# Four merged weight loads and an earlier turn of x tile 2 at the start of a linear-attention and mixer kernel

## The chip, the cores and the metric

The kernel runs on one core of a Trainium2 chip. The metric is the device time of one launch in microseconds (us); 1 KB is 1024 bytes. The profiled execution's span runs from its first to its last instruction. The core has five engines with a program each: TensorE (PE, with its weight loads shown apart as PEld), VectorE (DVE), ScalarE (ACT), GpSimd (POOL) and SyncE (SP). SP and ACT issue DMA transfers from queues of their own.

## The reference

Two blocks work on the same x (2048 tokens of 640 values) and are mixed by a gate. Only the first lines matter for the change.

```python
g = _sigmoid((x * gate_w).sum(-1, keepdims=True))
qkv = (x @ wqkv)                       # 640 -> 3 * 640, split into q, k, v; 32 heads of 20
phi = lambda t: jnp.where(t > 0, t + 1, jnp.exp(t)) + 1e-6
pq, pk = phi(q), phi(k)
kv = jnp.einsum("bhsd,bhse->bhde", pk, v)
num = jnp.einsum("bhqd,bhde->bhqe", pq, kv)
...
b = _B_ref(x, w1, w2, w3, w4)          # layernorm, w1, gelu, token shifts, w2, layernorm, w3, gelu, w4
return g * a + (1 - g) * b
```

## The kernel before

The tokens are cut into 16 tiles of 128. A weight matrix with 640 rows is held as five slices of 128 rows, k = 0 to 4. A product for a token tile is five accumulating matmuls, one for each slice, into a PSUM bank: the turned x tile (`xT`) is the loaded operand, the slice of `wq` (512 columns) or of `wkg` (512 columns and 130 more, which hold the rest of wk, a column of ones and a column of the gate) is the one streamed.

The loads at the start are listed one after another. `load_x` puts x tiles on SP's queue; `load_wq` and `load_wk` (L683 to L687) put one slice each on the queue that they are given. SP's order is x0, x1, wq2, x2, wk0, x3, wk2, wk4, x4, then the DMA transposes `x_turn(3)`, the load of x5, `x_turn(4)` and so on; ACT's is wq0, wq1, wq3, wq4, wk1, wk3, and the last 128 columns of wq ("the tail of wq"). L285 issues every plain transfer, L281 every DMA transpose. Each load has its own semaphore, and whatever reads a slice waits for the semaphore of the transfer that wrote it.

x tiles 0, 1 and 2 are turned on PE instead: `t_x` transposes five blocks of 128 columns into a PSUM bank (L615) and DVE copies them into `xT` (L669). For tile 2 a sixth small matmul (L604, 128x5) goes into the same bank, with the gate's column, and DVE copies that into `wkg`; the first copy of tile 2 comes after it.

PE first runs warm-up matmuls on constants (L884), then `t_x(0)`, one more warm-up, and the two step lists. `q_three` makes the q tiles 0 to 2 and `k_two` the k tiles 0 and 1. Their lists name (tile, slice) pairs in PE's order, and (t, None) is the turn of tile t. `stream` issues them at L922 (512 columns) and L923 (the 130 more). When a tile's last slice is done, `phi` evicts it: an Exp on ACT (L660) into one of three slots of `Er`, then two DVE operations (L626, L643). A k tile has two more ACT operations, a copy of its last two columns and a sum of squares. From k tile 2 on each tile is one group of matmuls, `k_tile` or `q_tile` (L604).

All work after this is ordered by a planner (`_Items.run`): it holds streams of items and takes the next item by its estimated time, by its own model of the engines. `q_three` and `k_two` are one item each. Each engine runs its own list strictly in that order.

Of the kernel before, what the change touches and what calls it, by code (L numbers as in the profile page):

```python
# [11 lines left out]
D = 640  # L12
# [404 lines left out]
def _build(nc, A_x, A_wqkv, A_wo, B_w1, B_w2, B_w3, B_w4, gate_w, out, dbg=None, stop=None):  # L417
    sch = _Sched(nc)
# [79 lines left out]
    wkg = ra.alloc("wkg", [128, KD, NK], BF16)  # L498
    wq = ra.alloc("wq", [128, KD, D], BF16)
# [18 lines left out]
    def bank():  # L518
        best = None
        for k_ in range(nbanks[0]):  # L520
            b = (bank_rr[0] + k_) % nbanks[0]
            if b in bank_pend or b in bank_hold:
                continue
            lk = sch.locks.get(b)
            tfree = 0.0 if lk is None else sch.ev_time.get((lk[1].sem, lk[1].val), 1e18)
            if best is None or tfree < best[0]:
                best = (tfree, b)
        bank_rr[0] = best[1] + 1
        bank_pend.add(best[1])
        return best[1]  # L530
# [4 lines left out]
    def pair():  # L535
        best = None
        for k_ in range(4):
            q_ = (bank_rr[0] // 2 + k_) % 4
            tf = 0.0
            ok = True  # L540
            for b in (2 * q_, 2 * q_ + 1):
                if b in bank_pend or b in bank_hold:
                    ok = False
                lk = sch.locks.get(b)
                if lk is not None:
                    tf = max(tf, sch.ev_time.get((lk[1].sem, lk[1].val), 1e18))
            if ok and (best is None or tf < best[0]):
                best = (tf, 2 * q_)
        b = best[1]
        bank_rr[0] = b + 2  # L550
        bank_pend.update((b, b + 1))
        return b
# [36 lines left out]
    def pe(fn, reads, writes, cost=500.0):  # L589
        for w_ in writes:  # L590
            sp_, rl = sch.rects(w_)
            if sp_ == "ps":
                for (_p0, _p1, lo, hi) in rl:
                    for b in range(lo // PS_BANK, (hi - 1) // PS_BANK + 1):
                        bank_pend.discard(b)
        return sch.op("pe", fn, reads, writes, cost=cost)
# [83 lines left out]
    def load_x(t):  # L680
        dma_in(x_tok[:, t, :], x2[128 * t:128 * (t + 1), :], "x%d" % t)

    def load_wq(k, queue):  # L683
        sch.dma(queue, wq[:, k, 0:512], A_wqkv[128 * k:128 * (k + 1), 0:512], "wq%d" % k)

    def load_wk(k, queue):
        sch.dma(queue, wkg[:, k, 0:D], A_wqkv[128 * k:128 * (k + 1), D:2 * D], "wk%d" % k)  # L687

    def x_turn(t):
        sch.dma("sp", xT[:, :, 128 * t:128 * (t + 1)], x_tok[:, t, :], "trx%d" % (t % 4), transpose=True)  # L690
# [1 line left out]
    gwr = xn[:, 1, 0:128]  # L692
    dve(lambda e: e.memset(gwr, 0.0), [], [gwr])
    load_x(0)
    load_wq(0, "act")
    load_x(1)
    load_wq(1, "act")
    load_wq(2, "sp")
    load_wq(3, "act")
    load_x(2)  # L700
    load_wq(4, "act")
    load_wk(0, "sp")
    load_wk(1, "act")
    load_x(3)
    load_wk(3, "act")
    sch.dma("act", wq[:, :, 512:D], A_wqkv[:, 512:D].rearrange("(k p) f -> p k f", p=128), "wqt")
    load_wk(2, "sp")
    load_wk(4, "sp")
    load_x(4)
    x_turn(3)  # L710
    load_x(5)
# [65 lines left out]
    def t_x(t):  # L777
        for k0, k1 in ((0, 1), (1, KD)) if t < 2 else ((0, KD),):
            b = bank()
            tr_group(b, [x_tok[:, t, 128 * k:128 * (k + 1)] for k in range(k0, k1)])  # L780
            if t == 2:
                mm_group(ps[:, b, 448:448 + KD], [(gwr, ident[:, 0:KD])])
            for j0, j1 in {(1, 1): ((1, 3), (3, KD)), (2, 0): ((0, 2), (2, KD))}.get((t, k0), ((k0, k1),)):
                copy(dve, xT[:, j0:j1, 128 * t:128 * (t + 1)], psb(b, 128 * (j0 - k0), 128 * (j1 - k0)).rearrange("p (k c) -> p k c", k=j1 - j0))
            if t == 2:
                copy(dve, wkg[:, :, D + 1:D + 2], ps[:, b, 448:448 + KD].rearrange("p (k o) -> p k o", o=1))

    def phi(b, dst, after_exp=None, n=D):
        se = slot("E", 3)
        src = psf[:, 512 * b:512 * b + n]  # L790
        er = Er[:, se, 0:n]
        activation(er, src, ACTF.Exp)
        if after_exp is not None:
            after_exp()
        ts(dve, er, er, 1.0, EPS_PHI, ALU.min, ALU.add)
        return stt(dst, src, 1.0 + EPS_PHI, er, ALU.add, ALU.max)
# [79 lines left out]
    def warmup(cols, cyc):  # L876
        b = bank()
        one = nc.const_aps.tensor(1.0, [128, 512], BF16)
        steps = [512] * (cols // 512) + [128] * (cols % 512 // 128)

        def fn(e):
            ins = None
            for n in steps:
                ins = e.matmul(ps[:, b, 0:n], one[:, 0:128], one[:, 0:n], start=True, stop=True)  # L884
            return ins
        pe(fn, [], [ps[:, b, :]], cost=cols * cyc)
# [19 lines left out]
    def stream(order, w, n2, done):  # L906
        bs = {}
        for t in sorted({t for t, k in order if k is not None}):
            bs[t] = pair() if n2 else bank()
            bank_hold.update((bs[t], bs[t] + 1) if n2 else (bs[t],))  # L910
        for t, k in order:
            if k is None:
                if t is None:
                    warmup(256, 0.42)
                else:
                    t_x(t)
                continue
            b = bs[t]
            l = xT[:, k, 128 * t:128 * (t + 1)]

            def fn(e, l=l, b=b, k=k):
                ins = e.matmul(ps[:, b, 0:512], l, w[:, k, 0:512], start=(k == 0), stop=(k == KD - 1))  # L922
                return ins if not n2 else e.matmul(ps[:, b + 1, 0:n2], l, w[:, k, 512:512 + n2], start=(k == 0), stop=(k == KD - 1))  # L923
            pe(fn, [w[:, k, 0:512 + n2], l], [ps[:, b, 0:512]] + ([ps[:, b + 1, 0:n2]] if n2 else []), cost=272.0 if n2 else 216.0)
            if k == KD - 1:
                bank_hold.difference_update((b, b + 1) if n2 else (b,))
                done(t, b)

    def q_three():
        order = [(0, 0), (1, None), (0, 1), (1, 0), (1, 1), (0, 2), (1, 2), (0, 3), (1, 3), (2, None), (0, 4), (1, 4),  # L930
                 (2, 0), (2, 1), (2, 2), (2, 3), (2, 4)]
        stream(order, wq, 0, lambda t, b: phi(b, pq_tok[:, t + 1, 0:512], n=512))

    def k_out(t, b):
# [1 line left out]
        activation(junk[:, 0, :], x_tok[:, t, :], ACTF.Square, accum=st1[:, 1, t:t + 1])  # L936

    def k_two():
        stream([(0, 0), (0, 1), (0, 2), (1, 0), (0, 3), (1, 1), (1, 2), (0, 4), (1, 3), (1, 4)], wkg, 130, k_out)

    def addA(name, dur, fn, deps=()):
        IT.add("A", name, dur, fn, deps)
# [2 lines left out]
    addA(("tx", 0), 0.28, lambda: t_x(0))  # L945
    addA(("warm", 1), 0.0, lambda: warmup(WARM2, 0.42))
    addA(("q", 2), 3.24, q_three)
    addA(("k", 1), 2.72, k_two)
    addA(("k", 2), 1.36, lambda: k_tile(2))
    for i in range(3, NT + 2):  # L950
# [449 lines left out]
    order = IT.run(sch, hook)  # L1400
# [6 lines left out]
def bass_gated_mix__linear_attn_block__mixer_s_mlp__prompt_kernel(  # L1407
    nc, A_x, A_wqkv, A_wo, B_x, B_w1, B_w2, B_w3, B_w4, gate_w, out
):
    assert tuple(A_x.shape) == (1, S, D) and tuple(out.shape) == (1, S, D)  # L1410
    assert tuple(A_wqkv.shape) == (D, 3 * D) and tuple(A_wo.shape) == (D, D)
    assert tuple(B_w1.shape) == (D, D) and tuple(B_w2.shape) == (D, D)
    assert tuple(B_w3.shape) == (D, F) and tuple(B_w4.shape) == (F, D) and tuple(gate_w.shape) == (D,)
    _build(nc, A_x, A_wqkv, A_wo, B_w1, B_w2, B_w3, B_w4, gate_w, out)
# [28 lines left out]
```

## Time and profile before

| What | Value |
|---|---|
| Time, median of 3 | 259.3 us (258.84 to 259.4) |
| Profiled execution, its own time | 259.2 us |
| Its span | 257.9 us |
| First matmul on x (transpose, L615) | 3.68 us |
| First q step (L922) | 4.38 us |
| First k step (L922) | 8.96 us |
| First ACT table load; first Exp | 4.14 us; 7.73 us |
| First x transpose by DMA on SP | 8.75 us |
| HBM read, written | 12.04 MB, 2.62 MB |

Times in views are counted from the span's start. A line of the timeline gives start, duration, engine, line of the code, operation, output<-inputs and, in brackets, the idle time before it and what ended it. The queues' lines (SPq, ACTq) show the issue of a transfer, not its data; the DMA issues give the time from an issue's start to its landing.

### The profile page before, as it was taken

To read this page: it belongs to the slowest core of one execution; us is meant where nothing else is said; L and a number is where in the kernel's file an instruction comes from. 1 tells how busy PE (TensorE), PEld (TensorE's weight loads), DVE (VectorE), ACT (ScalarE), POOL (GpSimd) and SP (SyncE) were. 2 spreads that over 40 slices of the span, in tenths; PEclk is the share of its full clock that TensorE was granted. 3 is DMA by queue.
4 is the path that set the end of the run, shared out by engine and by line. 5 is a ranking of instruction groups with operands and counts; after the bars stand their busy time and mean duration, and the time that the engine had idled before them with its cause. 6 is when DMAs were issued, how large, how long until landed. Compare 5 with 4: busy or idle time off the path is not lost.

```text
span 257.9 us, 3904 instructions
## 1 busy us (share of the span) xinstructions
PE 255.1 (99%) x1478; PEld 126.7 (49%) x1478; DVE 144.8 (56%) x289; ACT 108.9 (42%) x224; POOL 90.9 (35%) x144
## 2 busy tenths in 40 slices
PE   8999999999999999999999999999999999999996
PEld 4555555544454545555444445444444744444744
DVE  2697888899964995589999300399700033200033
ACT  1587676651366868666854331001540100253100
POOL 5020499976952162677908000123200021300000
PEclk9999999999999999999999999999999999999999
DMA  7856699956637699372628630114130022200012
GB/s 226 226 135 114 188 137 177 262 109 126 127 76 79 125 399 293 84 100 56 121 49 117 123 60 3 31 25 127 36 17 0 3 52 80 102 1 3 0 20 102
DMA packets 57650, 26.50 MB, mean 103 GB/s; under 512 B 48884, under 2 KB 56221, under 8 KB 57632
## 3 DMA queue, kind: packets, MB, share of 16 engines
q1 hardware_dynamic: 54800, 21.87, 40.2%
q0 software_dynamic: 1168, 3.28, 5.8%
q10 hardware_dynamic: 1664, 1.11, 1.4%
q8 instruction: 11, 0.18, 0.3%
q14 instruction: 7, 0.06, 0.1%
HBM read 12.04 MB, written 2.62 MB: 57 GB/s over the span
## 4 chain that ended last, share of the span: by engine, by line
PE 99%; DVE 0%; issue 0%
PE ps L604 53%; PE ps L1213 30%; PE ps L811 8%; PE ps L922 2%; PE ps L884 1%; PE ps L1240 1%; PE ps L1128 1%; PE ps L615 1%; PE ps L1009 0%; PE ps L1038 0%; PE ps L923 0%; DVE x_tok L643 0%
## 5 line engine op out<-in xcount | busy, mean ns | idle before, releaser
L604 PE MATMUL ps<-xnT,w 128*128 128x512 bf16 x360 | 81.3, 379 | 0.0
L643 DVE SCALAR_TENSOR_TENSOR x_tok<-ps,stg,abx 128x512 bf16<-128x512 f32 (+2 forms) x17 | 12.2, 718 | 81.4 <-PE ps L1213 81.3
L660 ACT ACTIVATE h2T<-ps 128x512 bf16<-128x512 f32 x52 | 30.6, 598 | 59.5 <-PE ps L604 59.5
L604 PEld LDWEIGHTS ps<-xnT,w 128*128 128x128 bf16 x360 | 34.5, 98 | 39.8 <-issue 0.5
L1213 PE MATMUL ps<-w,h2T 128*128 128x512 bf16 (+2 forms) x221 | 45.4, 366 | 0.0
L626 POOL TENSOR_SCALAR xn<-x_tok,st 128x640 bf16<-128x640 bf16 x32 | 36.0, 1130 | 25.4 <-DMA xnT<-xn 24.9
L626 POOL TENSOR_SCALAR abx<-x_tok,stg 128x640 f32<-128x640 bf16 x16 | 15.3, 965 | 70.7 <-DVE x_tok L643 70.7
L1213 PEld LDWEIGHTS ps<-w,h2T 128*128 128x128 bf16 x221 | 21.2, 98 | 23.5
L660 ACT ACTIVATE Er<-ps 128x512 bf16<-128x512 f32 (+1 forms) x36 | 23.0, 649 | 14.6 <-PE ps L604 10.3
L659 ACT ACTIVATE junk<-x_tok 128x640 bf16<-128x640 bf16 x32 | 23.6, 738 | 3.9 <-DVE x_tok L641 3.7
L660 ACT ACTIVATE hsT<-ps 128x512 bf16<-128x512 f32 (+1 forms) x32 | 19.0, 594 | 12.5 <-PE ps L604 12.0
L604 PE MATMUL ps<-w,hsT 128*128 128x512 bf16 (+1 forms) x160 | 23.7, 299 | 0.0
L604 PE MATMUL ps<-wkg,xT 128*128 128x130 bf16 (+1 forms) x140 | 21.4, 299 | 0.0
L641 DVE SCALAR_TENSOR_TENSOR x_tok<-ps,x_tok 128x640 bf16<-128x640 f32 x16 | 13.1, 821 | 11.2 <-PE ps L604 10.5
L604 PEld LDWEIGHTS ps<-w,hsT 128*128 128x128 bf16 x160 | 13.3, 98 | 12.3
L1213 PE MATMUL ps<-M_sb,pqnT 128*128 128x512 bf16 (+2 forms) x85 | 18.6, 367 | 0.0
L811 PE MATMUL ps<-pk_tok,x_tok 128*128 128x512 bf16 x80 | 17.8, 379 | 0.0
L604 PEld LDWEIGHTS ps<-wkg,xT 128*128 128x128 bf16 x140 | 11.9, 97 | 11.4
L1157 DVE TENSOR_TENSOR pq_tok<-pq_tok,dnr 128x300 bf16<-128x300 bf16 (+1 forms) x48 | 16.9, 405 | 0.5
L634 DVE TENSOR_TENSOR qprod<-qprod,pk_tok 128x640 f32<-128x640 f32 x13 | 16.3, 1252 | 0.4
L626 DVE TENSOR_SCALAR Er<-Er 128x512 bf16<-128x512 bf16 (+1 forms) x36 | 12.3, 341 | 6.9 <-ACT Er L660 6.2
L604 PE MATMUL ps<-wq,xT 128*128 128x512 bf16 x65 | 16.2, 379 | 0.0
(87 smaller groups left out, 243.8 us busy)
## 6 DMA issues: line engine op xcount, KB each, us to landing
w<-in_B_w_dram SPq DMA_DIRECT2D x1, 2160.0 KB, 8.1
w<-in_B_w_dram SPq DMA_DIRECT2D x1, 2080.0 KB, 15.2
out_dram<-x_tok SPq DMA_DIRECT2D x3, 640.0 KB, 3.2
w<-in_B_w_dram POOLq DMA_DIRECT2D x8, 160.0 KB, 6.4
x_tok<-in_A_x_dram SPq DMA_DIRECT2D x6, 160.0 KB, 3.7
x_tok<-in_A_x_dram SPq DMA_DIRECT2D x1, 960.0 KB, 5.3
wv<-in_A_wqkv_dram POOLq DMA_DIRECT2D x1, 800.0 KB, 5.7
x_tok<-in_A_x_dram SPq DMA_DIRECT2D x1, 640.0 KB, 4.6
```

What stands on the lines that cost most here:

```text
L604: ins = e.matmul(out_ap, l, r, start=(i == 0), stop=(i == n - 1))
L615: ins = e.transpose(o, s_, ident[:])
L626: return engf(lambda e: e.tensor_scalar(out_ap, in_ap, s1, s2, op0, op1), rd, [out_ap], cost=cost)
L634: return engf(lambda e: e.tensor_tensor(out_ap, a, b_, op), [a, b_], [out_ap], cost=cost)
L641: return dve(lambda e: e.scalar_tensor_tensor(out_ap, in0, scalar, in1, op0, op1, accum_out=accum), rd, [out_ap, accum], cost=cost + 70.0)
L643: return dve(lambda e: e.scalar_tensor_tensor(out_ap, in0, scalar, in1, op0, op1), rd, [out_ap], cost=cost)
L659: return act(lambda e: e.activation(out_ap, in_ap, func, bias=bias, scale=scale, accum_out=accum), rd, wr, cost=cost)
L660: return act(lambda e: e.activation(out_ap, in_ap, func, bias=bias, scale=scale), rd, wr, cost=cost)
L811: ins = e.matmul(o, l, r, start=(t0 + q_ == 0), stop=(t0 + q_ == NT - 1))
L922: ins = e.matmul(ps[:, b, 0:512], l, w[:, k, 0:512], start=(k == 0), stop=(k == KD - 1))
L1157: dve(lambda e, o=o, i0=i0, i1=i1: e.tensor_tensor(o, i0, i1, ALU.mult), [i0, dnr[:, 1, sd, :]], [o], cost=cost)
L1213: ins = e.matmul(o, l, r, start=first and i == 0, stop=last and i == len(prs) - 1, skip_group_check=True)
```

## The change

The two single-slice loaders become one loader over a range of slices, and the lists are changed. The transfers, in bytes, are the same. SP now issues x0, x1, x2, wk 0-1, x3, x4; ACT issues wq0, wq1, wq 2-3, wq4, wk 2-4, the tail of wq. The turn of x tile 2 stands after (1, 0) in `q_three`, where it stood after (1, 3), and both step lists take the slices in the order of the new loads.

```diff
-    def load_wq(k, queue):
-        sch.dma(queue, wq[:, k, 0:512], A_wqkv[128 * k:128 * (k + 1), 0:512], "wq%d" % k)
-
-    def load_wk(k, queue):
-        sch.dma(queue, wkg[:, k, 0:D], A_wqkv[128 * k:128 * (k + 1), D:2 * D], "wk%d" % k)
+    def load_w(dst, n0, n1, k0, k1, queue, key):
+        src = A_wqkv[128 * k0:128 * k1, n0:n1]
+        if k1 - k0 == 1:
+            sch.dma(queue, dst[:, k0, 0:n1 - n0], src, "%s%d" % (key, k0))
+        else:
+            sch.dma(queue, dst[:, k0:k1, 0:n1 - n0], src.rearrange("(k p) f -> p k f", p=128), "%s%d" % (key, k0))
+
+    def load_wq(queue, k0, k1):
+        load_w(wq, 0, 512, k0, k1, queue, "wq")
+
+    def load_wk(queue, k0, k1):
+        load_w(wkg, D, 2 * D, k0, k1, queue, "wk")
...
     load_x(0)
-    load_wq(0, "act")
+    load_wq("act", 0, 1)
     load_x(1)
-    load_wq(1, "act")
-    load_wq(2, "sp")
-    load_wq(3, "act")
+    load_wq("act", 1, 2)
     load_x(2)
-    load_wq(4, "act")
-    load_wk(0, "sp")
-    load_wk(1, "act")
+    load_wq("act", 2, 4)
+    load_wk("sp", 0, 2)
+    load_wq("act", 4, 5)
     load_x(3)
-    load_wk(3, "act")
+    load_wk("act", 2, 5)
     sch.dma("act", wq[:, :, 512:D], A_wqkv[:, 512:D].rearrange("(k p) f -> p k f", p=128), "wqt")
-    load_wk(2, "sp")
-    load_wk(4, "sp")
     load_x(4)
     x_turn(3)
     load_x(5)
...
     def q_three():
-        order = [(0, 0), (1, None), (0, 1), (1, 0), (1, 1), (0, 2), (1, 2), (0, 3), (1, 3), (2, None), (0, 4), (1, 4),
-                 (2, 0), (2, 1), (2, 2), (2, 3), (2, 4)]
+        order = [(0, 0), (1, None), (0, 1), (1, 0), (2, None), (1, 1), (2, 0), (2, 1), (0, 2), (0, 3), (1, 2), (1, 3),
+                 (2, 2), (2, 3), (0, 4), (1, 4), (2, 4)]
...
     def k_two():
-        stream([(0, 0), (0, 1), (0, 2), (1, 0), (0, 3), (1, 1), (1, 2), (0, 4), (1, 3), (1, 4)], wkg, 130, k_out)
+        stream([(0, 0), (0, 1), (1, 0), (1, 1), (0, 2), (0, 3), (0, 4), (1, 2), (1, 3), (1, 4)], wkg, 130, k_out)
```

## The prediction

> **What bounds the kernel now.** I read the busy times and the chain of waits first, then the stretches of the first microseconds, then the timeline and the DMA issues there, because everything that the diff touches ends at about 12 us.
>
> ```profile
> PE 255.1 (99%) x1478; PEld 126.7 (49%) x1478; DVE 144.8 (56%) x289; ACT 108.9 (42%) x224; POOL 90.9 (35%) x144
> ...
> PE 99%; DVE 0%; issue 0%
> ```
>
> TensorE (PE) is the bound from start to end, and the chain that ended last runs through it alone. So a microsecond in which PE stands still at the start is a microsecond at the end, and there is almost nothing to win: only PE's gaps can be taken out. The next view is the stretches while the first loads run (columns: PE, weight loads, DVE, ACT, POOL busy, clock, DMA share, GB/s).
>
> ```profile
> 2.50:5.00 2.50, 2.50 (x16) 1.48 (x15) 0.65 (x2) 0.86 (x1) 2.00 (x11) 1.00 1.02 334
> 5.00:7.50 2.50, 2.50 (x19) 1.38 (x18) 0.71 (x3) 0.42 (x1) 0.00 (x0) 1.00 1.04 359
> ```
>
> The 16 DMA engines are full (share 1.02 and 1.04) at 334 to 359 GB/s. The loads are thus limited by bytes in a queue, not by how many transfers they are cut into; what counts is the order of the bytes. The next lines are SP's issues in the timeline (start, duration), then the DMA issues, one transfer each, with us from issue to landing.
>
> ```profile
> 1.71 0.43 SPq L285 DMA_DIRECT2D wq<-in_A_wqkv_dram  x1
> 2.18 0.43 SPq L285 DMA_DIRECT2D x_tok<-in_A_x_dram  x1
> 3.13 0.43 SPq L285 DMA_DIRECT2D x_tok<-in_A_x_dram  x1
> 3.60 1.13 SPq L285 DMA_DIRECT2D wkg<-in_A_wqkv_dram  x2
> 4.77 0.58 SPq L285 DMA_DIRECT2D x_tok<-in_A_x_dram  x1
> ...
> wq<-in_A_wqkv_dram SPq DMA_DIRECT2D x1, 128.0 KB, 4.0
> x_tok<-in_A_x_dram SPq DMA_DIRECT2D x1, 160.0 KB, 4.3
> x_tok<-in_A_x_dram SPq DMA_DIRECT2D x1, 160.0 KB, 5.6
> wkg<-in_A_wqkv_dram SPq DMA_DIRECT2D x1, 160.0 KB, 5.8
> wkg<-in_A_wqkv_dram SPq DMA_DIRECT2D x1, 160.0 KB, 6.2
> x_tok<-in_A_x_dram SPq DMA_DIRECT2D x1, 160.0 KB, 6.0
> ```
>
> Issue plus landing time gives: wq slice 2 at 5.7, x tile 2 at 6.5, x tile 3 at 8.7, wk slice 2 at 9.4, wk slice 4 (issued at 4.1) at 10.3, x tile 4 at 10.8. The transfers land nearly in the order in which SP and ACT alternately issued them. Call each 128-row load a piece: x0, wq0, x1, wq1, wq2 (5th), wq3, x2, wq4, wk0, wk1, x3 (11th), wk3, wk2 (13th). From the 5th to the 13th that is (9.4 - 5.7) / 8 = 0.46 us a piece. Last, PE around the turn of x tile 2:
>
> ```profile
> 5.71 1.03 PE L922 MATMUL ps<-wq,xT 128*128 128x512 bf16 x4
> ...
> 7.01 0.44 PE L615 MATMUL ps<-ident,x_tok 128*128 128x128 bf16 x5
> 7.29 0.17 PE L604 MATMUL ps<-ident,xn 128*128 128x5 bf16 x1
> 7.32 0.59 PE L922 MATMUL ps<-wq,xT 128*128 128x512 bf16 x2
> 7.52 0.55 DVE L669 COPY xT<-ps 128x256 bf16<-128x256 bf16 x2 [1.49 <-PE ps L604]
> 7.53 0.73 PE L922 MATMUL ps<-wq,xT 128*128 128x512 bf16 x2
> 7.87 0.36 PEld L922 LDWEIGHTS ps<-wq,xT 128*128 128x128 bf16 x3 [0.45 <-DVE xT L669]
> ...
> 8.96 0.38 PE L922 MATMUL ps<-wkg,xT 128*128 128x512 bf16 x1
> ...
> 9.23 0.38 PE L922 MATMUL ps<-wkg,xT 128*128 128x512 bf16 x1
> ```
>
> A 512-column step takes (1.03 - 0.38) / 3 = 0.217 us of PE, a k step 9.23 - 8.96 = 0.27. The turn takes 7.29 - 7.01 = 0.28 for five transposes and 0.03 for the gate column. From the gate matmul it is 0.23 to the first copy and 0.35 from there to the weight load of (2, 0): 0.58 in all. Two steps, (0, 4) and (1, 4), stood in that time; the second, at 7.53, was through at 7.75, and the next began at 7.87: a stall of 0.12. From 8.96 on PE's starts follow each other at these paces.
>
> **The change, part by part.**
>
> *Four transfers fewer.* SP issues six loads before its first transpose where it had nine: 3 x 0.43 = 1.3 us of SP. That transpose waits for x tile 3 (8.7 us), so nothing moves; without that cover SP's later transposes would come up to 1.3 us sooner. ACT saves one issue of about 0.45; its table load at 4.1 us comes sooner, but its first Exp waits for PE at 7.7. Cost 0.
>
> *The turn of x tile 2 moves ahead.* Up to (1, 0), at 5.71, every operand is a load that keeps its place. Then comes the turn, at 5.71 + 0.22 = 5.93, if x tile 2 is there. It is now the 5th piece, in wq2's place: 5.7 + (32 KB more, at about 350 GB/s) 0.1 = 5.8. No stall at this value; between 5.7 and 6.1 the cost is 0 to 0.2. The gate matmul stands at 6.21 and (1, 1) at 6.24, through at 6.46. The next step is (2, 0), ready at 6.21 + 0.58 = 6.79. Only one step covers the copy where two did, so the stall is 0.33 against 0.12: **+0.21 us**. Nothing can be drawn past it, since PE's order is fixed: all later steps queue behind (2, 0).
>
> *wq 2 and 3 as one transfer.* Both are seen only when both landed. If each transfer gets its turn whole they are pieces 6 and 7: 6.5. If x, wq and wk pieces alternate, the second half comes after the first half of wk 0-1, as piece 8: 7.0. (2, 0) and (2, 1) hold PE to 6.79 + 0.43 = 7.22, and the weight load of (0, 2) can start at 7.0. Cost 0, 0.1 at the late end. Were x tile 2's two steps not there, the wait would be up to 0.5.
>
> *wq 4.* Piece 10 by the count: 8.2 (wk 1, the 10th before, landed there by the alternate order). Six steps from 7.22 end at 8.52, the load starts at 8.3. Cost 0, margin 0.1.
>
> *wk 0-1, then wk 2-4.* The q steps end three steps after 8.52, at 9.17 against 8.96. wk 0-1 are pieces 8 and 9 (7.8): no wait. Four k steps end at 9.17 + 4 x 0.27 = 10.25, so wk 2-4 must have landed by about 10.0. As pieces 12 to 14 they land at 9.4 + 0.46 = 9.9. From below they land at 9.4, if dropping the 256-byte tail of wq from among them helps; from above at 10.8, when x tile 4 did so far, since the same bytes are then through. Cost 0 to 0.8; I take 0, nearest to the count of pieces, with little to spare.
>
> *What follows on ACT and DVE.* The three q tiles now finish one step apart, at 8.52, 8.74 and 8.95, and their three evictions come in a row. Today the first Exp starts 0.41 after its last step (7.73 against 7.32) and takes 0.60, and DVE's starts for q tiles 0 and 1 are 0.93 apart (8.36, 9.29). So DVE begins at 8.52 + 0.41 + 0.60 = 9.5 and has three times 0.93 to do, to 12.3; k tile 0 was taken up at 12.09. That is 0.25 late, but k tile 1's Exp starts only at about 12.7, as it does now, and DVE has caught up by then. PSUM pairs for k tile 2 need q tile 1 out, at 11.5, against a PE that wants them at 11.9. Cost 0; without those 0.4 us PE would wait for DVE.
>
> *x tiles 3 and 4, the tail of wq, the rest.* x3 stays 11th; x4 lands a little sooner; all bytes are through at 11 as before, and the tail's first reader runs at 15.5. The planner sees other end times for the two step lists and may order later work otherwise; PE has no later gap to gain from, so I take 0, with 0.3 either way for the range.
>
> **A rule that speaks for it, and one against.** The rows say bytes, at 0.46 a piece. The Trainium skill, DMA: Bandwidth & Descriptors, "Rules for kernel authors", says to join many small transfers, as small ones are mostly overhead; its section on one DMA's anatomy puts the fixed part at about 2.0 us. By that rule alone four transfers fewer would be an estimated gain of up to 8 us of DMA time; a queue that is already full hides that part, so I give it nothing. The same page, "Queues, rings and completion order", says an engine changes between queues at packets, typically 9 to 17 descriptors; by it a three-slice load could be cut and x tile 4 let in, which an estimate puts at one piece, 0.46, later. That would make the sum about 0.3 more.
>
> **The sum.** +0.21 for the copy, 0 for the rest. The profiled execution had 257.9 us of span and 1.3 around it, 259.2, against a median of 259.3: the same within 0.1. So 259.3 + 0.2 = **259.5 us**, 0.1% up.
>
> **Rivals.**
> - *wk 2-4 arrive late* (slower). One semaphore for three slices holds k step 5 until the last byte. For: the margin is 0.1, and slice 4 alone took until 10.3. Against: the tail of wq no longer comes between. It decides from a landing at 10.3 on, when the wait of 0.3 and the 0.21 together pass 0.5. At 10.8 the wait is 0.8 and the time 260.3; in the middle 260.0.
> - *x tile 2 early feeds PE better* (a small gain). The stall goes, since DVE is idle before it, and the copy takes less. For: DVE waited 1.49 us. Against: nothing in the 0.58 is DVE queueing. If all of the 0.12 went, and the 0.08 ahead of the first q step (4.20 to 4.38 where a 128-column matmul needs 0.11): 259.1.
> - *The change does nothing*: later slack swallows 0.2. Against: PE has none. 259.3.
>
> **Chances.** The forecast 0.55, late wk slices 0.30, the small gain 0.07, nothing 0.08. About 0.2% (0.52 us) is what a measurement can tell from no change. The forecast, nothing and most of the small gain lie within it. Slower by more: 0.30 from the late slices and 0.06 of the forecast's spread. Faster by more: 0.06, for the three times shown alone lie 0.56 apart. So 0.06, 0.58 and 0.36. The range reaches from 259.0, under the small gain, to 260.3, the late slices' end.
>
> **What would show it.** Right: the turn's first transpose near 5.9, a gap of about 0.33 ahead of (2, 0), the first k matmul near 9.17, no gap ahead of the fifth k step, and equal paces after. Wrong: a wait on a weight load at (0, 2), (0, 4) or k slice 2, the landing of wk 2-4 after 10.0, or a gap after 14 us.

## The result and the profile after

| | us |
|---|---|
| before, median of 6 runs | 259.35 (258.84 to 259.87) |
| after, median of 6 runs | 260.49 (260.24 to 261.09) |
| after / before | 1.0040, 95% interval 1.0022 to 1.0057 |
| span, before and after | 257.9, 259.2 |
| forecast | 259.5 (259.0 to 260.3) |

The change made the kernel 1.1 us slower where the forecast was 0.2. On the chip some executions are disturbed as a whole; the medians from here on leave those out, so they can differ by a few hundredths from the ones that the recorded expectations quote. A ratio is given as it was measured, with its 95% interval; it is not the quotient of the two medians and can differ from it by up to 0.2%.

The page after, cut to span, busy times and the chain that ended last (shares of the span by engine):

```profile
span 259.2 us, 3872 instructions
...
PE 254.1 (98%) x1452; PEld 126.7 (49%) x1478; DVE 142.5 (55%) x289; ACT 108.8 (42%) x224; POOL 91.1 (35%) x144
...
PE 95%; DMA 2%; ACT 1%; issue 1%; SPq 0%; DVE 0%
```

The chain was PE alone at 99%. Now a transfer stands in it, at 2% of 259 us: it runs back from PE to a load of `x_tok` at the start, and further to that load's issue. The waits of the weight loads after (engine, line, releaser: total us, times, longest) name it:

```profile
PEld ps L615 <- DMA x_tok<-in_A_x_dram: 1.4, 1, 1.4
...
PEld ps L925 <- DVE xT L669: 0.5, 1, 0.5
...
PEld ps L925 <- DMA wq<-in_A_wqkv_dram: 0.2, 1, 0.2
```

L615 is the turn, so it is x tile 2. There is no wait on wk. The DMA issues at 1.7 us after, with KB and us from issue to landing:

```profile
wq<-in_A_wqkv_dram ACTq DMA_DIRECT2D x1, 256.0 KB, 6.4
x_tok<-in_A_x_dram SPq DMA_DIRECT2D x1, 160.0 KB, 5.2
```

x tile 2, issued at 1.71, landed at 6.87, and wq 2-3 at 8.09. The timeline after, from the last steps ahead of the turn (start, duration):

```profile
5.34 1.02 PE L925 MATMUL ps<-wq,xT 128*128 128x512 bf16 x2
...
6.91 0.28 PEld L615 LDWEIGHTS ps<-ident,x_tok 128*128 128x128 bf16 x5 [1.37 <-DMA x_tok<-in_A_x_dram]
6.92 0.45 PE L615 MATMUL ps<-ident,x_tok 128*128 128x128 bf16 x5 [0.55 <-DMA x_tok<-in_A_x_dram]
...
7.20 0.17 PE L604 MATMUL ps<-ident,xn 128*128 128x5 bf16 x1
...
7.23 0.38 PE L925 MATMUL ps<-wq,xT 128*128 128x512 bf16 x1
...
7.78 0.11 PEld L925 LDWEIGHTS ps<-wq,xT 128*128 128x128 bf16 x2 [0.48 <-DVE xT L669]
7.79 0.82 PE L925 MATMUL ps<-wq,xT 128*128 128x512 bf16 x3 [0.18 <-DVE xT L669]
...
8.13 0.19 PEld L925 LDWEIGHTS ps<-wq,xT 128*128 128x128 bf16 x2 [0.24 <-DMA wq<-in_A_wqkv_dram]
```

Read from the last line up: the weight load of (0, 2) waits 0.24 for wq 2-3 at 8.1, but it runs ahead of its matmul and PE does not stop. (2, 0) starts at 7.79, where (1, 1), begun at 7.23, needs 0.22: a gap of 0.34, the copy of x tile 2. The turn's first transpose is at 6.92, where (1, 0), begun at 5.77, was through at 5.99: 0.93 lost. (The 0.55 in brackets is less because ends of matmuls are modelled.) The first k matmul comes at 10.17 instead of 8.96: 1.21 later, and the last matmul of the kernel is 1.22 later (256.92 against 255.70). All that the change costs in this profile arises ahead of 8 us and is carried to the end unchanged.

### The profile page after: what moved, and what is told of

It is laid out like the page before. It is cut to its first block, busy times and chain, and to the rows that moved or that the text cites. A ratio compares the mean times of both kernels' runs of the same rounds, so it can differ in the third digit from the quotient of the medians.

```text
span 259.2 us, 3872 instructions
## 1 busy us (share of the span) xinstructions
PE 254.1 (98%) x1452; PEld 126.7 (49%) x1478; DVE 142.5 (55%) x289; ACT 108.8 (42%) x224; POOL 91.1 (35%) x144
## 3 DMA queue, kind: packets, MB, share of 16 engines
q10 hardware_dynamic: 1904, 1.41, 1.7%
## 4 chain that ended last, share of the span: by engine, by line
PE 95%; DMA 2%; ACT 1%; issue 1%; SPq 0%; DVE 0%
PE ps L604 51%; PE ps L1216 30%; PE ps L814 8%; DMA x_tok<-in_A_x_dram 2%; PE ps L925 2%; PE ps L1243 1%; ACT hsT L660 1%; PE ps L1131 1%; PE ps L1012 0%; PE ps L1041 0%; ACT junk L659 0%; SPq L285 0%; PE ps L926 0%; PE ps L615 0%; DVE x_tok L643 0%
## 5 line engine op out<-in xcount | busy, mean ns | idle before, releaser
L604 PE MATMUL ps<-xnT,w 128*128 128x512 bf16 x349 | 79.9, 379 | 0.5 <-issue 0.2
L1216 PE MATMUL ps<-w,h2T 128*128 128x512 bf16 (+2 forms) x216 | 44.7, 366 | 0.3
L604 PE MATMUL ps<-w,hsT 128*128 128x128 bf16 (+1 forms) x159 | 23.5, 298 | 0.2
L641 DVE SCALAR_TENSOR_TENSOR x_tok<-ps,x_tok 128x640 bf16<-128x640 f32 x16 | 13.1, 821 | 10.9 <-PE ps L604 10.3
L634 DVE TENSOR_TENSOR qprod<-qprod,pk_tok 128x640 f32<-128x640 f32 x13 | 15.1, 1164 | 0.4
```

Of the source, the lines that this page charges most:

```text
L604: ins = e.matmul(out_ap, l, r, start=(i == 0), stop=(i == n - 1))
L634: return engf(lambda e: e.tensor_tensor(out_ap, a, b_, op), [a, b_], [out_ap], cost=cost)
L641: return dve(lambda e: e.scalar_tensor_tensor(out_ap, in0, scalar, in1, op0, op1, accum_out=accum), rd, [out_ap, accum], cost=cost + 70.0)
L1216: ins = e.matmul(o, l, r, start=first and i == 0, stop=last and i == len(prs) - 1, skip_group_check=True)
```

## The experiments

Three theories of the loss were set against each other. O: the order costs it, that is the place of x tile 2 and the shorter cover of its copy. M: the joined transfers hold things back. C: chance, since loads land differently from execution to execution.

**One part at a time.** First the changed kernel again, for its spread.

> The changed kernel unaltered, for its profile a second time. In its first profile the first k matmul came 1.21 us later than in the kernel before: 0.99 of it because x tile 2, needed at 5.9, landed at 6.9, and 0.22 because only one step covers its copy. Theory O (order): x tile 2 takes the place in the queue in which some DMA engines always lag, so the late landing returns: x tile 2 at 6.4 to 7.0 again, 1.0 to 1.3 us slower than before, about 260.5. Theory C (chance of one profile): x tile 2 lands near 5.8 this time, a gap of at most 0.2 ahead of its turn, and the slower time has its place elsewhere.

Measured: 261.67 (lowest 259.76) against 259.66 for the kernel before, run beside it, ratio 1.0074 (1.0043 to 1.0104). x tile 2 landed at 7.37 in its profile, the copy gap was 0.34, the first k matmul at 10.68. Two more gaps of 0.95 and 0.97 came at 94 and 96 us, where PE waited for DVE's L641. The median holds such later losses too, so it says little of the start.

Then wq 2 and 3 apart again, all else as in the changed kernel:

```diff
-    load_wq("act", 2, 4)
+    load_wq("act", 2, 3)
+    load_wq("act", 3, 4)
```

> The changed kernel with wq slices 2 and 3 as two transfers again, one after the other on ACT's queue; all else as changed. Theory M (merging): the transfer of two slices makes the DMA engines lag, so x tile 2 lands near 5.8 here and the kernel is only some 0.2 to 0.3 us slower than before (259.6). Theory O (order): nothing is gained by it, x tile 2 lands at 6.4 to 7.0 and the time stays 1.0 to 1.3 us above before (260.4 to 260.6).

Measured: 260.92 (seven runs, lowest 259.71), ratio 1.0040 (1.0015 to 1.0065). x tile 2 landed at 6.31 and the first k step came at 9.61, a whole us sooner than in the run beside it; but the same late gaps (0.99 and 0.97 at 93 and 95 us) hid that in the time. The start speaks for M; a second effect muddles the time.

The other half, the kernel before with only the wk slices joined and their k order:

```diff
-    load_wk(0, "sp")
-    load_wk(1, "act")
+    load_wk(0, 2, "sp")
     load_x(3)
-    load_wk(3, "act")
+    load_wk(2, 5, "act")
...
-    load_wk(2, "sp")
-    load_wk(4, "sp")
```

> The kernel before with only the wk slices joined (0-1 on SP, 2-4 on ACT) and the k steps in their new order; wq, x tile 2 and the q steps stay as before. Theory M: joined loads make the engines lag; wq 3 or wk land late and PE waits 0.5 us or more, 259.9 to 260.5. Theory O: wk 2-4 land at about 9.9, needed at 9.8 here, so 0 to 0.2 us: 259.3 to 259.6, and x tile 2 lands at 6.5 as before.

Measured: 260.01 (six runs), ratio 1.0014 (0.9985 to 1.0042): by its interval not told from before.

And the order alone, with every load single:

```diff
-    load_wq(2, "sp")
-    load_wq(3, "act")
     load_x(2)
+    load_wq(3, "act")
+    load_wq(2, "sp")
...
-        order = [(0, 0), (1, None), (0, 1), (1, 0), (1, 1), (0, 2), (1, 2), (0, 3), (1, 3), (2, None), (0, 4), (1, 4),
-                 (2, 0), (2, 1), (2, 2), (2, 3), (2, 4)]
+        order = [(0, 0), (1, None), (0, 1), (1, 0), (2, None), (1, 1), (2, 0), (2, 1), (0, 2), (0, 3), (1, 2), (1, 3),
+                 (2, 2), (2, 3), (0, 4), (1, 4), (2, 4)]
```

> The kernel before with no transfer joined, but x tile 2 loaded ahead of wq slices 2 and 3 and the q steps in their new order (the turn after (1, 0)). Theory O: this is the whole loss: x tile 2 lands at 6.4 to 7.0, PE waits for it, 1.0 to 1.3 us slower than before (260.4 to 260.6). Theory M: x tile 2 lands near 5.8 and the kernel is 0.2 us slower (259.5), as was predicted for the change.

Measured: 259.86 against 259.66, ratio 1.0002 (0.9987 to 1.0018). x tile 2 landed at 6.18, the copy gap was 0.34, the first k step at 9.48. The order alone is no 1.1 us.

**A control, and the other parts.** The kernel before, as if it were a new one:

> The kernel before unaltered, for a second profile of it beside the others on the same chip. So far x tile 2 landed at 6.2 to 6.3 us where it was the third load on SP and wq 2 and 3 were apart, at 6.9 and 7.4 where they were joined; wq slice 2, the third load on SP in the kernel before, landed at 5.7. In the four runs on this chip PE also stood 1.7 to 6.8 us at 45 to 96 us in three kernels with joined wk loads, not in the one without. If that later loss comes from joined wk loads, this profile has no gap after 10 us and lasts 259 to 260 us; if it is the chip's, it has one here too. Third load on SP: 5.7 to 6.3.

Measured: 259.76 against 259.66, ratio 1.0003 (0.9975 to 1.0032). Its profile was the surprise of the study: 260.42 us, as slow as the changed kernel's. The waits of this second profile of the kernel before:

```profile
PEld ps L922 <- DMA wq<-in_A_wqkv_dram: 1.5, 1, 1.5
...
PE ps L922 <- DMA wq<-in_A_wqkv_dram: 1.2, 1, 1.2
...
PEld ps L615 <- DMA x_tok<-in_A_x_dram: 0.6, 1, 0.6
```

The unchanged kernel can wait 1.2 us too, for wq 2, which landed at 6.99 where the first profile had 5.70; its first k step came at 10.19. Its transfers from 4.0 to 6.5 us (the columns as in the stretches shown before: PE, weight loads, DVE, ACT, POOL, clock, DMA share, GB/s):

```profile
4.00:6.50 2.50, 1.85 (x14) 0.93 (x12) 1.36 (x5) 1.28 (x1) 0.71 (x5) 1.00 0.87 219
```

The same stretch of the changed kernel's first profile, and of the first profile of before:

```profile
4.00:6.50 2.50, 2.37 (x14) 1.10 (x11) 1.36 (x5) 1.03 (x1) 0.73 (x5) 1.00 0.86 224
...
4.00:6.50 2.50, 2.50 (x16) 1.39 (x15) 1.36 (x5) 1.28 (x1) 0.72 (x5) 1.00 1.01 334
```

The DMA engines are 86 to 87% busy and move 219 and 224 GB/s in the first two; the first profile of before had a share of 1.01 and 334 GB/s there. The pace of the loads at this place thus differs from execution to execution of one kernel, and one profile of each kernel can't tell M from C. From here on medians and several profiles count.

The changed kernel with wk single and the k order of before, so that of the transfers only wq 2-3 is joined:

```diff
-    load_wk("sp", 0, 2)
+    load_wk("sp", 0, 1)
     load_wq("act", 4, 5)
+    load_wk("act", 1, 2)
     load_x(3)
-    load_wk("act", 2, 5)
+    load_wk("act", 3, 4)
...
+    load_wk("sp", 2, 3)
+    load_wk("sp", 4, 5)
```

> The changed kernel with the wk slices single, in the queues and k steps of the kernel before; wq 2-3 stay joined and the turn stays early. It differs from the run order alone only by the joined wq 2-3. Theory M (the joined wq transfer holds x tile 2 back): x tile 2 lands at 6.7 to 7.4, the first k matmul comes at 10.0 to 10.7, 1.0 to 1.5 us slower than before (260.4 to 261.0). Theory O (the place in the queue alone): 6.1 to 6.3, first k matmul at 9.5, 0.2 to 0.6 us slower. If joined wk loads cause the later gaps, there is none here.

Measured: 260.43 against 259.66, ratio 1.0014 (0.9987 to 1.0041); none of its 10 runs under 259.89, where 18 of the 24 beside it are. x tile 2 at 6.86, first k step at 10.16, no gap later.

The changed loads with the old q order:

```diff
-        order = [(0, 0), (1, None), (0, 1), (1, 0), (2, None), (1, 1), (2, 0), (2, 1), (0, 2), (0, 3), (1, 2), (1, 3),
-                 (2, 2), (2, 3), (0, 4), (1, 4), (2, 4)]
+        order = [(0, 0), (1, None), (0, 1), (1, 0), (1, 1), (0, 2), (1, 2), (0, 3), (1, 3), (2, None), (0, 4), (1, 4),
+                 (2, 0), (2, 1), (2, 2), (2, 3), (2, 4)]
```

> The changed kernel with its loads as they are but the q steps in the order of the kernel before (the turn after (1, 3)). PE then needs wq slices 2 and 3, which landed at 8.1 to 8.2 in the changed kernel, where it is through with (1, 1) at about 6.4. If the loss lies in the loads, this is worse still: PE stands for some 1.7 us at (0, 2), the first k matmul comes near 10.7, 1.6 to 2.0 us slower than before. If the early turn itself is the loss, it is 0 to 0.3 us slower.

Measured: 262.86 (four runs), ratio 1.0108 (1.0027 to 1.0189). This is 3.2 us over before, where the expectation had 1.6 to 2.0: wq 2-3 landed at 8.85, PE stood 3.0 us at (0, 2) and not 1.7, and the clock fell, which the expectation left out. The stretches around it:

```profile
5.00:7.50 2.50, 0.87 (x5) 0.27 (x3) 0.62 (x3) 0.03 (x1) 0.00 (x0) 1.00 0.92 293
7.50:10.00 2.50, 1.10 (x3) 0.43 (x4) 0.00 (x0) 0.00 (x0) 0.00 (x0) 0.59 0.90 298
10.00:12.50 2.50, 2.50 (x12) 1.19 (x11) 0.70 (x4) 0.69 (x2) 0.00 (x0) 0.50 0.49 111
12.50:15.00 2.50, 2.50 (x10) 1.00 (x9) 1.82 (x4) 0.99 (x2) 0.00 (x0) 0.55 0.56 132
```

The seventh number is the granted clock: 0.59, 0.50, 0.55. So the new order is needed with the new loads; without it the joined slices are the second thing that PE asks for.

The kernel before with the turn one step earlier, so that three steps cover the copy:

```diff
-        order = [(0, 0), (1, None), (0, 1), (1, 0), (1, 1), (0, 2), (1, 2), (0, 3), (1, 3), (2, None), (0, 4), (1, 4),
+        order = [(0, 0), (1, None), (0, 1), (1, 0), (1, 1), (0, 2), (1, 2), (0, 3), (2, None), (1, 3), (0, 4), (1, 4),
```

> The kernel before with the turn of x tile 2 one step earlier, ahead of (1, 3), all loads as before: three steps of 0.22 us cover the copy (0.58 us) in place of two. If what was read of the copy is right, the gap of 0.12 ahead of (2, 0) goes. x tile 2 is needed at 6.6 and landed at 6.5 before, so up to 0.5 may be lost again where it lands later. 0.1 us faster to 0.4 slower; 259.2 if it lands in time.

Measured: 259.76, ratio 0.9991 (0.9965 to 1.0017). PE's gap at (2, 0) was gone in its profile; x tile 2 landed at 7.21 there, later than needed, and 0.1 us can't be seen in the time.

**The join by itself.** All loads single, x tile 2 ahead, wq 2 and 3 both on ACT: the run with wk single, with the diff of the second experiment on top.

> The changed kernel with wq 2 and 3 as two loads, both on ACT, and all wk slices single in the places and the k order of before: no joined transfer is left, what remains is the place of x tile 2, the move of wq 2 from SP to ACT, and the order of the q steps. Theory 'joined wq' (one 256 KB transfer beside x tile 2 makes it late): median 0.1 to 0.3 us over before, as the order alone had (259.86 against 259.72), x tile 2 landing near 6.2, first k matmul near 9.5. Rival 'place in the queues' (x tile 2 on SP shares the engines with whatever ACT has queued, and ACT now carries both slices): 0.6 to 0.9 over before, as with wk apart (260.42 against 259.66), x tile 2 landing near 6.9, first k matmul near 10.1.

Measured: 259.92 against 259.80, ratio 0.9999 (0.9975 to 1.0024). This is nearly the execution that the forecast described. Its timeline around the turn (the step lists are at L929 here):

```profile
5.36 0.89 PE L929 MATMUL ps<-wq,xT 128*128 128x512 bf16 x2
...
5.89 0.47 PEld L615 LDWEIGHTS ps<-ident,x_tok 128*128 128x128 bf16 x5 [0.34 <-DMA x_tok<-in_A_x_dram]
6.09 0.44 PE L615 MATMUL ps<-ident,x_tok 128*128 128x128 bf16 x5
...
6.40 0.38 PE L929 MATMUL ps<-wq,xT 128*128 128x512 bf16 x1
...
6.95 1.68 PE L929 MATMUL ps<-wq,xT 128*128 128x512 bf16 x7 [0.18 <-DVE xT L669]
```

x tile 2 landed at 5.85 (forecast 5.8), the turn's transposes start 0.09 after (1, 0), begun at 5.78, is through at 6.00 (too little to stand in brackets), and the main loss is 6.95 - 6.40 - 0.22 = 0.33 at (2, 0). The first k step came at 9.35, forecast 9.17.

> The same kernel with wq 2 and 3 joined again (a repeat of the run with wk apart, so that both stand on one chip and beside the same runs of before). Both theories: 0.6 to 0.9 us over before, no run much above that, x tile 2 landing at 6.9. A third theory, chance (the slow stretch of the loads between 4 and 6.5 us falls as it likes, as it did in the profile of before run as a control): this run and the one with wq apart are alike within 0.3.

Measured: 260.00, ratio 1.0020 (0.9982 to 1.0059); x tile 2 at 6.16. Here the join cost 0.08 in the medians, which is inside the noise: this pair alone spoke for chance.

> The changed kernel, unchanged, beside the other two. If joining the wk slices costs nothing at the start and only now and then later (the gaps of 1 us behind late transposes by DMA near 93 to 96 us in two profiles), its lowest runs are level with those of the run with wk apart (about 0.6 to 0.9 over before) and its upper ones 2 us and more higher. If the joined wk slices also cost at the start, the lowest runs are 0.3 higher as well.

Measured: 260.42, ratio 1.0030 (1.0004 to 1.0056); x tile 2 at 6.62, first k step at 9.92, no late gap. 0.42 over the run with wk single, its lowest runs (259.37, 259.63) level with that one's (259.44, 259.59).

**The join once more, without the late DMA transposes.** The same pair, each DMA transpose replaced by a plain copy of its bytes, so that late waits behind the transposes can't blur the start. These kernels leave out the turns of x tiles 3 to 15 and of later tensors, so their outputs mean nothing; only their times are used.

```diff
             if transpose:
-                return e.dma_start_transpose(out_ap, in_ap)
+                if len(out_ap.shape) == 3:
+                    in_ap = in_ap.rearrange("p (k f) -> p k f", f=out_ap.shape[2])
+                return e.dma_start(out_ap, in_ap)
```

> The kernel before, with each of its 71 DMA transposes written as a plain copy of the same bytes (so the turns of x tiles 3 to 15 and of the later tensors are left out); the first of them waits for x tile 3 at 8.7 us, so the start up to the first k step is the same program. It is the base of the next three. Its time can differ from that of before by a few us, as a copy of 256-byte rows is another load on the queues. Fifth load (wq 2) anywhere from 5.7 to 7.0, first k matmul 3.05 to 3.26 us after it.

Measured: 259.74 against 259.62 for the real kernel before, ratio 0.9998 (0.9980 to 1.0016). The copies change nothing that can be measured, so the base holds.

> The same with x tile 2 ahead, wq 2 and 3 apart on ACT, wk single (the kernel that gave 259.92), its DMA transposes left out in the same way. Theory 'joined wq': x tile 2 at 5.8 to 6.3, 0 to 0.3 us over the base. Chance: a landing up to 7.3 here too. Both: if x tile 2 lands after 6.0, the first k matmul 3.30 us after it; a gap of 0.34 at (2, 0).

Measured: 259.68, ratio 1.0005 (0.9995 to 1.0015).

> The same with wq 2-3 joined, and nothing else changed. Joined theory: x tile 2 at 6.6 to 7.4, the median 0.3 us or more over that with wq apart. Chance: the medians within 0.2. Both: first k matmul 3.30 us after x tile 2.

Measured: 260.52, ratio 1.0036 (1.0024 to 1.0048). Eleven of the 12 runs with wq apart end at 259.89 or less and the last at 260.46; all 12 with wq joined lie from 260.03 to 261.12. The timeline around the turn with wq apart:

```profile
6.13 0.45 PE L617 MATMUL ps<-ident,x_tok 128*128 128x128 bf16 x5 [0.60 <-DMA x_tok<-in_A_x_dram]
...
6.45 0.38 PE L931 MATMUL ps<-wq,xT 128*128 128x512 bf16 x1
...
7.00 1.47 PE L931 MATMUL ps<-wq,xT 128*128 128x512 bf16 x6 [0.18 <-DVE xT L671]
```

And with wq joined:

```profile
7.31 0.45 PE L617 MATMUL ps<-ident,x_tok 128*128 128x128 bf16 x5 [1.02 <-DMA x_tok<-in_A_x_dram]
...
7.63 0.38 PE L930 MATMUL ps<-wq,xT 128*128 128x512 bf16 x1
...
8.19 0.39 PE L930 MATMUL ps<-wq,xT 128*128 128x512 bf16 x1 [0.18 <-DVE xT L671]
```

Both have the same 0.55 to 0.56 from (1, 1) to (2, 0). The difference is the wait ahead of the turn: it starts at 6.13 in the one and at 7.31 in the other.

The join moved to SP's queue, behind x tile 2:

```diff
-    load_wq("act", 2, 4)
-    load_wk("sp", 0, 1)
     load_wq("act", 4, 5)
+    load_wq("sp", 2, 4)
+    load_wk("act", 0, 1)
     load_wk("act", 1, 2)
```

> The same with wq 2-3 joined on SP's queue right behind x tile 2, and wq 4, wk 0 and wk 1 as single loads on ACT meanwhile. If a joined load beside x tile 2 is what makes it late, x tile 2 lands at 5.9 to 6.3, the median is 0 to 0.3 over the base and at least 0.2 under that of the joined load beside it. Chance: a landing anywhere from 5.8 to 7.3, medians alike within 0.2.

Measured: 260.53, ratio 1.0042 (1.0025 to 1.0059). x tile 2 landed at 6.30, as M expected; the time was no better, and the profile shows why:

```profile
7.22 0.60 PE L930 MATMUL ps<-wq,xT 128*128 128x512 bf16 x2 [0.18 <-DVE xT L671]
...
7.99 0.33 PEld L930 LDWEIGHTS ps<-wq,xT 128*128 128x128 bf16 x3 [0.65 <-DMA wq<-in_A_wqkv_dram]
7.99 0.60 PE L930 MATMUL ps<-wq,xT 128*128 128x512 bf16 x2 [0.16 <-DMA wq<-in_A_wqkv_dram]
```

(2, 1), begun at 7.45, is through at 7.67 and (0, 2) starts at 7.99: 0.32 lost to the joined slices themselves, which landed at 7.94. The expectation that the time would fall back missed this: a good part of the wait only changed its place. In the profiles the first k step came at 9.94, against 9.39 with wq apart: 0.32 of it from here and 0.22 from x tile 2.

> The kernel with x tile 2 ahead, wq 2 and 3 apart and wk single, its DMA transposes left out, once more: 0 to 0.3 us over before, as the run before had (259.68 against 259.66). x tile 2 at 5.8 to 6.3; if after 6.0, the first k matmul 3.30 us after it.

Measured: 259.82 against 259.71, ratio 1.0009 (0.9991 to 1.0027); x tile 2 at 5.97.

> The same with wq 2-3 joined, once more. Joined theory: 0.3 us or more over the run with wq apart of this call (0.85 in the call before). Chance: within 0.2.

Measured: 260.29, ratio 1.0010 (0.9998 to 1.0022); x tile 2 at 6.88. The median is 0.47 over that of the run with wq apart; the two ratios don't differ.

> The changed kernel, its DMA transposes left out in the same way, so that the late gaps behind them can't hide the start: it differs from the run with wq joined only in the joined wk loads and the k order. If the joined wk loads cost nothing at the start, its median is within 0.2 of that run; if they do, 0.3 or more above it, with a wait at the first k step or at k slice 2, or x tile 2 later still.

Measured: 260.62, ratio 1.0044 (1.0024 to 1.0064); x tile 2 at 6.42, first k step at 9.76, no wait on wk. 0.33 over the run before it.

## Why the prediction was wrong, point by point

All profiles with the early turn, by what is joined (us from the span's start):

| Joined | x tile 2 landed, one profile each | mean |
|---|---|---|
| nothing, or wk alone | 5.85, 5.97, 6.08, 6.18, 6.31 | 6.08 |
| wq 2-3 beside it, wk single | 6.16, 6.86, 6.88, 7.26 | 6.79 |
| wq 2-3 beside it, wk joined | 6.42, 6.62, 6.87, 7.37 | 6.82 |

*The step that failed* is the landing of x tile 2: "It is now the 5th piece, in wq2's place: 5.7 + (32 KB more, at about 350 GB/s) 0.1 = 5.8. No stall at this value; between 5.7 and 6.1 the cost is 0 to 0.2." It landed at 6.87, and the term put at 0 cost 0.93. With the joined load beside it, it never landed within those bounds, in eight profiles; without it, in three of five. Behind it stands the reading that "the loads are thus limited by bytes in a queue, not by how many transfers they are cut into". The bytes were the same and the cut mattered. The early turn depends on that landing directly: in seven of these eight profiles the first k matmul stands 3.30 to 3.34 us after it, in the eighth 3.45 (wq 2-3 cost 0.13 at (0, 2) there). The turn started at 6.92 where 5.93 was forecast, 0.99 late, and that is 1.00 at the k steps: forecast 9.17, measured 10.17.

*How much of it is the join.* Of the 40 ways to set one of the five profiles without the joined load against one of the eight with it, 38 have the later landing with the join. In time it is less clear. In three pairs that differ in nothing but the join of wq 2-3 the medians lie 0.08, 0.84 and 0.47 apart and the ratios 0.0021, 0.0031 and 0.0001 (0.55, 0.81 and 0.03 us), always to the side of the join; only in the second pair do the intervals part. A fourth pair, the first two experiments, gave 0.75 with the late gaps in it. The single loads cost 0.20, 0.12, 0.06 and 0.11 over before (order alone, then wq apart on ACT three times), none of it clear of the noise. So O falls and M holds, and C sets how much of it one execution shows. The changed kernel itself lay 1.14, 2.01 and 0.62 over before, and 0.91 with the copies, so the 1.1 of the result is one draw.

A late landing also happens without any join: wq 2, a single load in the same place of SP's queue, landed between 5.70 and 6.99 in the old order. The landing goes by the pace of all loads and by the part of it that SP's queue gets. The join shows in the second. These are the bytes that the two queues moved from 4.5 to 5.5 us, with wq apart and then joined, in the pair without DMA transposes (packets, MB, share of the engines' time). q1 is SP's and q10 ACT's: q10's total grows from 1.11 MB in the page before to 1.41 after, by the 288 KB that moved to ACT.

```profile
q1 hardware_dynamic: 103, 0.12, 56.0%
q10 hardware_dynamic: 90, 0.08, 27.9%
...
q1 hardware_dynamic: 91, 0.10, 49.2%
q10 hardware_dynamic: 134, 0.13, 43.9%
```

SP's queue, which brings x tile 2 there, had 60% of these bytes with wq apart and 44% with wq joined. By the bytes in the traces it had 52 to 64% in all ten profiles with wq 2 and 3 apart, 25 to 45% in all nine with them joined on ACT, and 58% with them joined on SP's own queue. So a joined load on ACT's queue takes a larger part of the DMA engines just while x tile 2 is due. The landing records of the transfers, which come in sixteen parts, show it from the other side. For x tile 2, in the same pair:

```
            1st    8th    12th   last
wq apart    4.59   5.09   5.26   6.08
wq joined   4.61   5.23   5.73   7.26
```

The first eight parts come at almost the same time. The tile waits for the last ones. The Trainium skill, DMA: Bandwidth & Descriptors, "Why a DMA increments its semaphore by 16 and not by 1", says that up to 16 DMA engines finish a transfer independently and only the full count means landed; the sixteen parts here agree, from 4.61 to 7.26. Why the engines divide their time so beside a joined load was not settled. The same page, "Queues, rings and completion order", lets an engine finish a whole packet of one queue before it turns to the other, and a joined load has 256 rows where a single one has 128; no run here shows the packets of a single engine in order. The join also lets ACT issue what follows sooner (wq 4 at 2.20 instead of 2.67 in this pair). No run takes that apart, though ACT had issued all its loads by 4.2 us in both.

*The pace had a lucky source.* The 0.46 us a piece came from the profile with the most GB/s between 4.0 and 6.5 us of all in this study (334; the others 199 to 328). In the four profiles of the old order with all loads single (one has the turn a step earlier) the first k step came at 8.96, 9.30, 9.30 and 10.19, mean 9.44; with the new order and wq apart at 9.34, 9.35, 9.39, 9.48 and 9.61, mean 9.43. That fits how little the copy's 0.21 shows in the medians of the single loads: three of the four old ones came 0.34, 0.34 and 1.23 after the profile shown before, having waited for wq 2 and x tile 2, and that one happened not to.

*The copy of x tile 2: +0.21.* Right. A gap of 0.33 was forecast; it was 0.34 in the changed kernel, and 0.33 or 0.34 in all other profiles with the early turn.

*wq 2 and 3 as one transfer: 6.5 to 7.0.* Landed at 8.09, and at 7.41 to 8.33 in the other profiles with the early turn and the join beside it. The cost on PE was 0 all the same, because the late turn had moved the need for it to the same place; where x tile 2 came at 6.30, the join cost 0.32 by itself, and in one profile with the join beside it 0.13. The forecast counted its waits from where a weight load could start, here and for wk 2-4; the 0.24 that the weight load of (0, 2) waited cost PE nothing.

*wk 2-4 late* (the slower rival). It landed at 10.93, 1.0 later than forecast and past the 10.3 from which it was to decide. PE was late by as much, and its fifth k step didn't wait. The rival reached the right side by the wrong mechanism. Joining wk may still cost: the medians lie 0.42 and 0.33 over the same kernel with wk single, neither clear of the spread of the runs. No profile shows where; x tile 2 lands no later for it (6.82 against 6.79) and there is no wait on wk. That stays open.

*x tile 3 stays 11th, SP's transposes stay.* Wrong: it landed at 9.65 instead of 8.74, and SP's first transpose started at 9.66 instead of 8.75. Nothing on PE waited for it in the result's profile. The gaps near 93 to 96 us in two later profiles may have come from there; with them absent in others of the same kernel this wasn't settled.

*ACT, DVE, the planner: 0.* Right: the loss at the first k step, 1.21, is that at the last matmul, 1.22.

*The other rivals.* A small gain and no effect both fell: the wait of DVE was never the limit, and PE has no slack. Of the signs named for a wrong forecast two came, a wait at (0, 2) and wk 2-4 after 10.0, and neither cost PE anything; the cost was in a load that the list did not name, x tile 2.

*The rule for joining*, to which the forecast gave nothing, hardly reaches these loads. The Trainium skill, DMA: Bandwidth & Descriptors, "Rules for kernel authors", says that transfers under 64 KB are mostly overhead; each load that was joined here has 128 KB or more. The fixed 2.0 us stand in that page's section for transfers issued from GpSimd, and these come from SP and ACT. In the runs joining two loads cost time.

## What to carry to other kernels

A wait at the start of a kernel bound by one engine is paid in full at the end (1.21 us at the first k step was 1.22 at the last matmul), so loads that the first steps ask for are better kept apart, with a semaphore each, than joined: here 128 KB against 256. Joining two of them saves an issue, which nobody waited for. It makes the second slice's bytes the condition of the first, and here it took a part of the engines from the load on the other queue that PE needed next. Before the landing times of one profile become the terms of a sum, take a second profile of the same kernel: here it moved a landing by 1.3 us.

## What the runs showed of the hardware

- The same loads of the same kernel moved 334 GB/s in one execution and 219 in another between 4.0 and 6.5 us, with the DMA engines 101% and 87% busy. Every profile had a slower stretch there, of different depth, and about 350 GB/s again by 7.5 us. What causes it wasn't tried.
- One part of sixteen can hold a transfer: in the third profile of the changed kernel fifteen parts of x tile 2 had landed by 5.25 and the last came at 6.62.
- A PE that stood idle for 3.0 us came back at half the clock (0.50 to 0.59 in the stretches up to 15 us, shown with the old q order); with 1.0 us idle by the same view, in the joined run without DMA transposes, it stayed at 1.00. The mean of 0.59 from 7.50 to 10.00 is a full clock up to about 7.95 and half from there, so the clock fell some 2.1 us after PE's last matmul, which ended at 5.87. The Trainium skill, TensorE: Matmul & The Clock Gate, "Part 1: The HAM clock gate (the 'warmup' mystery)", puts the return to half rate at an idle window of some 3.4 us; here less was enough.
